# One add moved to VectorE, and GpSimd's work put in another order, in a hash-masked attention followed by a PReLU layer

## The chip, the cores and the metric

The kernel runs on one core of a Trainium2 chip. The metric is the device time of one launch in microseconds (us). A profile is one execution recorded by the hardware; its span runs from the first to the last instruction, and the launch's time is a little longer. The engines are named as in the profile: PE (TensorE, matrix products), DVE (VectorE), ACT (ScalarE), POOL (GpSimd), SP (SyncE, which here only starts transfers).

## What is computed

Attention with a hash mask, then a two-layer network with a PReLU between its products. Everything is float32.

```python
# q, k, v: (4, 8, 768, 64), proj: (64, 6)
q_bits = (einsum('bhsd,dk->bhsk', q, proj) > 0)
k_bits = (einsum('bhsd,dk->bhsk', k, proj) > 0)
mask   = bucket(q_bits)[:, :, :, None] == bucket(k_bits)[:, :, None, :]
scores = where(mask, q @ k.T / sqrt(64), -1e9)
attn   = softmax(scores)                # rows sum to 1
x      = (attn @ v) as (3072, 512)      # heads side by side
# w_in: (512, 2048), w_out: (2048, 512), alpha: (2048,)
h = x @ w_in
g = maximum(h, 0) + alpha * minimum(h, 0)
out = g @ w_out
```

## The kernel before

**The two parts.** `fast_path` has an attention part, up to about 336 us of the profile, and a dense part after it, where the two products are done with seven instead of eight block products each. The change is in the attention part alone.

**Attention by pairs.** The 32 heads of the batch are taken as 16 pairs (`NPAIR`), and the loop `for pi in range(NPAIR)` does one pair in each turn. The 768 keys are six tiles of 128 (`kc` from 0 to 5), the queries two groups of 384 columns (`g`), so that a pair has twelve cells. For a cell TensorE adds a product of the bits (bf16) and one of k and q (float32) into PSUM (L763), and ScalarE writes its exponential into the key tile `pts[kc]` (L766). There are only six such tiles, used anew by each pair. After the twelve cells TensorE multiplies them by v (`attend`, L796).

**The sums of the softmax.** The denominators are sums over all keys. The six key tiles, 1536 columns each, are first added together elementwise: `add_first` puts tiles 0 and 1 into `accp` (DVE, L774), `add_third` adds tile 2 to it (POOL, L782), `add_last` puts tiles 3, 4 and 5 into `accd` (DVE, L778 and L779), and `add_total` adds `accp` to `accd` (DVE, L785). Then `totals` multiplies `accd` by ones on TensorE (the tile `sm`, L810), which sums over the partitions. `divide` is called in the next pair's turn: DVE transposes the totals (L826), takes reciprocals into `rr` (L829), copies four blocks of 32 partitions by 12 columns between the quarters of the partitions (L832, L833), and, after a break in which `weight_begin` runs (clamp and shift of a piece of weights, L606 and L612, and `add_first`, L774), spreads the reciprocals by a transpose (`dn`, L837), multiplies (L843), and sends the result `x` to DRAM (`x_s`).

**The bits.** `hash_bits(pi + 1)` is called in pair `pi`'s turn: TensorE multiplies q and k by `proj` (L725), ScalarE takes the sign (L731), and six transfers issued from POOL's queue (L736, L738) bring the signs to the partitions where the next pair's scores want them.

**The weights.** Between these steps the weights are rounded, piece by piece, two pieces to a pair: ACT takes absolute values (L596, L600), DVE clamps (L606), shifts (L612), joins the sign (L637) and adds (L640). Four pieces of `w_in` make a group in a tile `wsi` with two buffers, and each group needs four sums of blocks (`weight_group`, POOL, L658), and then four transfers to DRAM (`w_in_s`, SP, L663). The sums and the store are put into the list `sums_due`, from which `weight_sums(count)` takes as many sums as its argument says, and a store where one comes first. It is called once in a pair, after `add_total`, with 2. There are four groups, so 16 sums; by the trace they run in pairs 3, 4, 6, 7, 9, 10, 12 and 13.

**Order.** Every engine works through its own queue in order. `do(...)` keeps an instruction in program order on its engine. Transfers aren't kept so: in pairs 9 and 12 the two sums stand between the bits' transfers in POOL's queue, in the other pairs ahead of all six.

Of the kernel before, what the change touches and what calls it, by code (L numbers as in the profile page):

```python
# [8 lines left out]
F32 = mybir.dt.float32  # L9
# [4 lines left out]
ALU = mybir.AluOpType  # L14
# [393 lines left out]
def fast_path(  # L408
# [13 lines left out]
    P = 128  # L422
# [20 lines left out]
    do = tc.keep_in_program_order  # L443
    PE, DVE, ACT, POOL = nc.tensor, nc.vector, nc.scalar, nc.gpsimd

    const = ctx.enter_context(tc.tile_pool(name="const", bufs=1))
# [8 lines left out]
    NPAIR = len(pairs)  # L455
# [25 lines left out]
    accp, accd, av, vsum, sums = {}, {}, {}, {}, {}  # L481
# [120 lines left out]
    def weight_clamp(i):  # L602
        if i < NW:
            i = order[i]
            x = wx[i]
            do(DVE.tensor_scalar(x, x, HI_MIN, None, op0=ALU.max, op1=ALU.max, accum_out=wmax[:, i : i + 1]))  # L606

    def weight_parts(i):
        i = order[i]
        x = wx[i].bitcast(U32)  # L610
        turned = i < HW and i % 4 == 3
        do(DVE.tensor_scalar(  # L612
            x, x, 3, 0x40000000 if turned else 0xC0000000, op0=ALU.logical_shift_left, op1=ALU.bitwise_xor,
        ))
# [27 lines left out]
    sums_due = []  # L642
# [24 lines left out]
            sums_due.append((one, (x[0], x[1], ALU.subtract, x[2])))  # L667
        sums_due.append((store, ()))

    def weight_sums(count):  # L670

        while sums_due and count:
            fn, x = sums_due.pop(0)
            count -= fn.__name__ == "one"
            fn(*x)


    def two_banks(name):
        return psum.tile([P, 2, 512], F32, name=name, tag="sc", bufs=3)
# [28 lines left out]
    def hash_bits(pi, halves=BOTH, engine=None):  # L708

        if halves.start == 0:
            bits["q", pi] = qbs[pi % 2]
            kb = pool.tile([P, 3 * CW], BF16, name=f"kb{pi}", tag="kb", bufs=1)
            bits["k", pi] = kb[:, :S]
            bits["raw", pi] = kb.rearrange("p (a w) -> p a w", w=CW)
        ps = {"k": two_banks(f"hs{pi}")}
        ps["q"] = psum_av.tile([P, 2, 512], F32, name=f"hsq{pi}", tag="av") if engine is DVE else ps["k"]
        for half in range(halves.start, halves.stop):
            for name in "qk" if engine is DVE else "kq":  # L720
                for s in range(2):
                    r, c = D * s, D * (s ^ half) + 32 * "kq".index(name)

                    for t, c in [("k", c)] + ([("q", c ^ D)] if engine is DVE and name == "q" else []):
                        do(PE.matmul(  # L725
                            ps[t][c : c + 32, half if t == "k" or engine is not DVE else 0, :CW], wh[r : r + D],
                            tr[name, pi][r : r + D, half * CW : (half + 1) * CW], start=True, stop=True,
                        ))
        if engine is None:
            raw = bits["raw", pi]  # L730
            do(ACT.activation(raw[:, 0:3:2], ps["k"][:, :, :CW], AF.Sign, bias=hb))  # L731
            for half in range(2):
                for s in range(2):
                    c = D * (s ^ half)
                    cols = slice(half * CW, (half + 1) * CW)
                    nc.gpsimd.dma_start(bits["q", pi][D * s : D * s + 32, cols], raw[c + 32 : c + 64, 2 * half])  # L736
                    if half:
                        nc.gpsimd.dma_start(bits["k", pi][D * s : D * s + D, cols], raw[c : c + D, 2])  # L738
            return
        for half in range(halves.start, halves.stop):  # L740
            cols = slice(half * CW, (half + 1) * CW)
            for s in range(2):
                c = D * (s ^ half ^ (engine is DVE)) + 32
                do(ACT.activation(
                    bits["q", pi][D * s : D * s + 32, cols], ps["q"][c : c + 32, 0 if engine is DVE else half, :CW], AF.Sign, bias=hb[c : c + 32],
                ))

            for to, c, n in [(0, 0, P)] if half == 0 else [(0, D, D), (D, 0, D)]:
                dst, src = bits["k", pi][to : to + n, cols], ps["k"][c : c + n, half, :CW]
                do(DVE.tensor_scalar(  # L750
                    dst, src, hb_k[c : c + n, 0:1], hb_k[c : c + n, 1:2], op0=ALU.is_gt, op1=ALU.subtract,
                ))
# [16 lines left out]
    def p(kc):  # L769
        return pts[kc].rearrange("p g s w -> p (g s) w")[:, :, :CW]  # L770

    def add_first(pi):
        accp[pi] = pool.tile([P, 2 * NCH, CW], F32, name=f"accp{pi}", tag="accp", bufs=1)
        do(DVE.tensor_tensor(accp[pi], p(0), p(1), op=ALU.add))  # L774
# [4 lines left out]
        do(DVE.tensor_tensor(accd[pi], accd[pi], p(5), op=ALU.add))  # L779

    def add_third(pi):
        do(POOL.tensor_tensor(accp[pi], accp[pi], p(2), op=ALU.add))  # L782

    def add_total(pi):
        do(DVE.tensor_tensor(accd[pi], accd[pi], accp[pi], op=ALU.add))  # L785
# [29 lines left out]
    def divide(pi, between=lambda: None):  # L815

        b, hp = pairs[pi]
        n = HW2 // 32  # L820
        a = pool.tile([P, NCH, HW2], F32, name=f"st{pi}", tag="st", bufs=1)
        r = pool.tile([P, NCH, n], F32, name=f"rc{pi}", tag="rc")
        rr = pool.tile([P, NCH, 2, n], F32, name=f"rr{pi}", tag="rr")
        d = pool.tile([P, NCH, CW], F32, name=f"dn{pi}", tag="dn", bufs=1)
        for g in range(NCH):
            do(DVE.transpose(a[:, g], sums[pi][:, g, :HW2]))  # L826
        do(DVE.tensor_scalar(r, a.rearrange("p g (n w) -> p g n w", w=32)[:, :, :, 0], S * EPS, None, op0=ALU.add))
        for h in range(2):
            do(DVE.reciprocal(rr[:, :, h], r))  # L829
        for q0 in (0, D):  # L830
            q1 = q0 + 32
            do(DVE.tensor_copy(rr[q0 : q0 + 32, :, 1], rr[q1 : q1 + 32, :, 1]))  # L832
            do(DVE.tensor_copy(rr[q1 : q1 + 32, :, 0], rr[q0 : q0 + 32, :, 0]))  # L833
        vsum[pi] = pool.tile([P, 1], F32, name=f"vs{pi}", tag="vs")
        do(DVE.tensor_scalar(vsum[pi], av[pi][:, 0, CW : CW + 1], EPS, None, op0=ALU.mult))
        between()
        do(DVE.transpose(  # L837
            d.rearrange("p g w -> p (g w)"),
            rr.rearrange("p g h n -> p (g h n)").unsqueeze(2).to_broadcast([P, 2 * NCH * n, 32]),
        ))  # L840

        x = mid.tile([P, NCH, CW], F32, name=f"x{pi}", tag="x", bufs=1)
        do(DVE.scalar_tensor_tensor(x, av[pi][:, :, :CW], vsum[pi], d, op0=ALU.add, op1=ALU.mult))  # L843
        nc.sync.dma_start(x_s[b, hp], x.rearrange("p g w -> p (g w)"))
# [316 lines left out]
    for pi in range(NPAIR):  # L1161
        i = 2 * pi

        def weight_begin():
            weight_clamp(i)
            weight_parts(i)
            add_first(pi)

        scores(pi, [c for c in CELLS if pi or c not in ahead])
        if pi:  # L1170
            divide(pi - 1, weight_begin)
        else:
            add_first(pi)
        weight_sum(i)
        weight_group(i)
        load_weight(i + 3)
        if pi == 0:
            weight_abs(1, DVE)
        weight_clamp(i + 1)
        add_third(pi)  # L1180
        add_last(pi)
        weight_parts(i + 1)
        weight_sum(i + 1)
        weight_group(i + 1)
        load_weight(i + 4)
        add_total(pi)
        weight_sums(2)
        if pi + 1 < NPAIR:
            hash_bits(pi + 1)
            if pi:  # L1190
                do(ACT.activation(tr["q", pi + 1], tr["q", pi + 1], AF.Copy, scale=DOWN))
        if pi + 2 < NPAIR:
            for name in "qk":
                (turn_blocks if name in BY_BLOCKS else turn)(pi + 2, name)
        attend(pi)
        if pi + 1 == NPAIR:
            now = ff1(0, 0)
            now.step(1)
        totals(pi)
        if pi + 1 == NPAIR:  # L1200
            now.step(5)
            divide(pi)
        else:
            weight_abs(i + 2)
        if pi + 2 < NPAIR:
            load(pi + 2, "v")
        if pi in (9, 11, 15):
            load_w((9, 11, 15).index(pi))
        if pi in (9, 10, 12):
            load_x(0, *{9: (0,), 10: (2, 3), 12: (1,)}[pi])  # L1210
        if 11 <= pi < 14 or pi == 15:
            sum_x(0, min(pi - 11, 3), DVE)
        if pi == 1:
            setup_alpha()
        for name in "qk":
            magnitude(pi, name)
            if pi + 3 < NPAIR:
                load(pi + 3, name)
        if pi + 1 < NPAIR:
            weight_abs(i + 3)  # L1220
# [97 lines left out]
```

## Time and profile before

| | us |
|---|---|
| median of 3 runs (891.02 to 896.54) | 891.14 |
| the profiled execution | 891.28 |
| its span | 889.4 |
| attention part, about | 336 |

| group (line, engine, what) | count | busy us | mean ns |
|---|---|---|---|
| L774 DVE, tiles 0 and 1 | 16 | 28.1 | 1758 |
| L782 POOL, tile 2 | 16 | 51.1 | 3194 |
| L778, L779 DVE, tiles 3 to 5 | 32 | 61.3 | 1963 and 1870 |
| L785 DVE, the total | 16 | 28.0 | 1751 |
| L658 POOL, sums of w_in | 16 | 29.3 | 1834 |
| L637 DVE, sign of the weights | 32 | 42.3 | 1322 |
| L736, L738 POOL, transfers of the bits | 90 | | about 500 each to issue |

The table's groups are sums over the whole span. [...] A row of the timeline gives start, duration, engine, line, operation, output and inputs with their shapes, the count, and in brackets the idle time before it with what ended it.

### The profile page before, as it was taken

The numbers are of one execution on the slowest core, as the hardware profiler recorded it, in microseconds if no ns is written. First come the engines' busy times: TensorE is split into PE (matmuls) and PEld (weight loads), VectorE is DVE, ScalarE is ACT, GpSimd is POOL, SyncE is SP. The second block draws the span as 40 slices with busy tenths as digits, with TensorE's granted clock in tenths as the row PEclk, the third lists the DMA queues.
The fourth block names the chain that finished last, engine by engine and source line by source line (L and its number), as shares of the span: only waits on it lengthen the run. The fifth ranks groups of instructions, "written<-read, shape, count | busy, mean of one in ns | idle before, by whom it ended". The sixth has DMA issues, their size and how long they took to land.

```text
span 889.4 us, 15185 instructions
## 1 busy us (share of the span) xinstructions
PE 864.7 (97%) x5718; PEld 577.0 (65%) x5718; DVE 766.4 (86%) x1262; ACT 370.1 (42%) x654; POOL 140.7 (16%) x152
## 2 busy tenths in 40 slices
PE   9999999998999999999999999999999999999996
PEld 4444444444444445558996558997557997557996
DVE  6999999998999987899898768898668988668986
ACT  7777677786787753221112222112222112222111
POOL 2334424434436311210000000000000000000000
PEclk9999999999999999999999999999999999999998
DMA  8665876867787616688334435434435343520242
GB/s 214 157 156 133 238 169 159 215 144 211 211 233 183 203 48 219 194 298 294 108 119 117 143 118 157 146 107 124 148 116 162 111 145 86 176 93 1 95 158 60
DMA packets 167683, 137.23 MB, mean 154 GB/s; under 512 B 122880, under 2 KB 151248, under 8 KB 164016
## 3 DMA queue, kind: packets, MB, share of 16 engines
q1 hardware_dynamic: 160000, 123.64, 47.6%
q0 software_dynamic: 5184, 11.34, 3.7%
q10 hardware_dynamic: 2416, 1.18, 0.5%
q8 instruction: 47, 0.77, 0.4%
q14 instruction: 36, 0.29, 0.1%
HBM read 104.87 MB, written 28.31 MB: 150 GB/s over the span
## 4 chain that ended last, share of the span: by engine, by line
PE 71%; DVE 12%; ACT 6%; issue 4%; DMA 3%; POOL 3%; SPq 0%; DVEq 0%; ACTq 0%; POOLq 0%
PE sc L763 7%; ACT pt L766 5%; PE av L796 4%; PE f_0a L896 2%; PE z_4a L896 2%; PE z_7a L896 2%; PE z_3a L896 2%; PE z_6a L896 2%; PE z_5a L896 2%; PE f_4a L896 2%; PE f_3a L896 2%; PE f_2a L896 2%; PE f_1a L896 2%; PE z_2a L896 2%; PE f_5a L896 2%
## 5 line engine op out<-in xcount | busy, mean ns | idle before, releaser
L766 ACT ACTIVATE pt<-sc 128x768 f32<-128x768 f32 x192 | 155.0, 812 | 42.0 <-PE sc L763 41.9
L763 PE MATMUL sc<-qT,kT 64*128 64x384 f32 x768 | 155.6, 483 | 0.0
L796 PE MATMUL av<-pt,vn 128*32 128x385 f32 (+1 forms) x1536 | 127.4, 486 | 0.0
L796 PEld LDWEIGHTS av<-pt,vn 128*32 128x32 f32 x1536 | 48.7, 109 | 77.4 <-issue 68.7
L763 PEld LDWEIGHTS sc<-qT,kT 64*128 64x128 f32 x768 | 69.1, 187 | 41.3 <-issue 39.9
L782 POOL TENSOR_TENSOR accp<-accp,pt 128x1536 f32<-128x1536 f32 x16 | 51.1, 3194 | 164.1 <-DVE accp L774 164.1
L763 PE MATMUL sc<-qb,kb 64*128 64x384 bf16 x384 | 64.9, 324 | 5.8 <-DMA qb<-kb 4.4
L949 DVE TENSOR_TENSOR g<-g,g 128x384 f32<-128x384 f32 x128 | 68.4, 555 | 2.2
L1013 DVE TENSOR_TENSOR gs<-g,gs 128x768 f32<-128x768 f32 x56 | 53.3, 952 | 1.0
L1005 DVE TENSOR_TENSOR ws<-wl 128x512 f32<-128x512 f32 x56 | 38.5, 687 | 18.1 <-DMA wl<-w_out_s 17.0
L1013 DVE TENSOR_TENSOR gs<-g 128x768 f32<-128x768 f32 x56 | 53.3, 951 | 0.0
L637 DVE SCALAR_TENSOR_TENSOR wx<-raw,wx 128x512 uint32<-128x512 uint32 x32 | 42.3, 1322 | 0.5
L945 DVE SCALAR_TENSOR_TENSOR g<-h,alpha 128x384 f32<-128x384 f32 x32 | 19.7, 616 | 25.2 <-ACT h L938 25.1
L763 PEld LDWEIGHTS <-kb 64*128 64x128 bf16 x384 | 20.0, 94 | 30.9 <-issue 4.6
L596 ACT ACTIVATE wr<-raw 128x512 int32<-128x512 uint32 x32 | 22.4, 701 | 32.4 <-issue 23.7
L774 DVE TENSOR_TENSOR accp<-pt,pt 128x1536 f32<-128x1536 f32 x16 | 28.1, 1758 | 8.5 <-ACT pt L766 8.2
L736 POOL DMA_DIRECT2D qb<-kb x60 | 30.2, 506 | 23.0 <-ACT kb L731 20.5
L779 DVE TENSOR_TENSOR accd<-accd,pt 128x1536 f32<-128x1536 f32 x16 | 29.9, 1870 | 2.0 <-ACT wr L596 0.5
L778 DVE TENSOR_TENSOR accd<-pt,pt 128x1536 f32<-128x1536 f32 x16 | 31.4, 1963 | 0.0
L658 POOL TENSOR_TENSOR wsi<-wsi 128x512 f32<-128x512 f32 x16 | 29.3, 1834 | 8.5 <-DVE wsi L640 8.0
L785 DVE TENSOR_TENSOR accd<-accd,accp 128x1536 f32<-128x1536 f32 x16 | 28.0, 1751 | 0.0
L896 PE MATMUL f_0a<-x,wi 128*128 128x384 f32 x64 | 23.5, 489 | 0.0
(352 smaller groups left out, 1749.8 us busy)
## 6 DMA issues: line engine op xcount, KB each, us to landing
wi<-w_in_s SPq DMA_DIRECT2D x32, 896.0 KB, 4.8
wl<-w_out_s SPq DMA_DIRECT2D x16, 1024.0 KB, 4.8
wl<-w_out_r SPq DMA_DIRECT2D x12, 1024.0 KB, 5.0
raw<-in_moe_w_out_dram SPq DMA_DIRECT2D x16, 512.0 KB, 4.6
raw<-in_moe_w_in_dram SPq DMA_DIRECT2D x16, 512.0 KB, 4.1
w_in_s<-wsi SPq DMA_DIRECT2D x16, 448.0 KB, 5.3
vn<-in_v_dram SPq DMA_DIRECT2D x16, 384.0 KB, 5.3
x_s<-x SPq DMA_DIRECT2D x16, 384.0 KB, 2.5
```

What stands on the lines that cost most here:

```text
L637: do(DVE.scalar_tensor_tensor(x.bitcast(U32), hi, 0x80000000, x.bitcast(U32), op0=ALU.bitwise_and, op1=ALU.bitwise_xor,))
L736: nc.gpsimd.dma_start(bits["q", pi][D * s : D * s + 32, cols], raw[c + 32 : c + 64, 2 * half])
L763: do(PE.matmul(sc[:, s, :CW], what["k", pi][r, ks], what["q", pi][r, qs], start=first, stop=not first,))
L766: do(ACT.activation(pts[kc][:, g, :, :CW], sc[:, :, :CW], AF.Exp, scale=SCALE / DOWN))
L778: do(DVE.tensor_tensor(accd[pi], p(3), p(4), op=ALU.add))
L779: do(DVE.tensor_tensor(accd[pi], accd[pi], p(5), op=ALU.add))
L782: do(POOL.tensor_tensor(accp[pi], accp[pi], p(2), op=ALU.add))
L796: do(PE.matmul(av[pi][D * s + t : D * s + t + 32, g, :w], nat["v", pi][:, s, kc * D + t : kc * D + t + 32], pts[kc][:, g, s, :w], start=(k ...
L896: do(PE.matmul(self.ps[bank], self.left(left, k), self.right(right, k), start=start and k == 0, stop=k == self.nk - 1, skip_group_check=no ...
L949: do(DVE.tensor_tensor(new_g(b, to)[:, i], g_m[b, x][:, i], g_m[b, y][:, i], op=ALU.subtract))
L1005: do(DVE.tensor_tensor(t, w2[b, n, x], w2[b, n, y], op=op))
L1013: do(DVE.tensor_tensor(t, g2[b, n, x], g2[b, n, y], op=ALU.subtract))
```

## The change

Three things are changed. Tile 2 of the keys is added to `accp` by VectorE instead of GpSimd. The four small copies of reciprocals go from VectorE to GpSimd. And the sums of `w_in` are taken one at a time, at two places: one after `hash_bits`, with a copy of one column of the pair's total (`late_sum`) put ahead of it, so that GpSimd doesn't begin before the total is there; the other in the next pair's `divide`, behind the copies of the reciprocals.

```diff
+    late_sum = const.tile([P, 1], F32, name="late_sum")
+
+    def weight_sums(count, after=None):
+
+        if sums_due and after is not None:
+            do(POOL.tensor_copy(late_sum, after[:, 0, :1]))
         while sums_due and count:
             fn, x = sums_due.pop(0)
             count -= fn.__name__ == "one"
             fn(*x)
...
     def add_third(pi):
-        do(POOL.tensor_tensor(accp[pi], accp[pi], p(2), op=ALU.add))
+        do(DVE.tensor_tensor(accp[pi], accp[pi], p(2), op=ALU.add))
...
         for q0 in (0, D):
             q1 = q0 + 32
-            do(DVE.tensor_copy(rr[q0 : q0 + 32, :, 1], rr[q1 : q1 + 32, :, 1]))
-            do(DVE.tensor_copy(rr[q1 : q1 + 32, :, 0], rr[q0 : q0 + 32, :, 0]))
+            do(POOL.tensor_copy(rr[q0 : q0 + 32, :, 1], rr[q1 : q1 + 32, :, 1]))
+            do(POOL.tensor_copy(rr[q1 : q1 + 32, :, 0], rr[q0 : q0 + 32, :, 0]))
+        weight_sums(1)
         vsum[pi] = pool.tile([P, 1], F32, name=f"vs{pi}", tag="vs")
...
         add_total(pi)
-        weight_sums(2)
         if pi + 1 < NPAIR:
             hash_bits(pi + 1)
+        weight_sums(1, accd[pi])
+        if pi + 1 < NPAIR:
             if pi:
                 do(ACT.activation(tr["q", pi + 1], tr["q", pi + 1], AF.Copy, scale=DOWN))
```

In the queues this gives: VectorE has 16 more adds of 1536 columns and 64 fewer copies; `add_third` stands on it between the second clamp (L606) and L778. GpSimd's queue has, for each pair, the six transfers of the bits, then `late_sum` and a sum, the four copies, a sum. The transfers on SP's queue are the same, with those of `w_in_s` about one pair later, and TensorE's and ScalarE's queues are the same. The lines named in the prediction are those of the kernel before.

More of the change, by code (lines that the diff above doesn't have):

```diff
@@ L668, in weight_group @@
         sums_due.append((store, ()))
-    def weight_sums(count):
+    late_sum = const.tile([P, 1], F32, name="late_sum")
+    def weight_sums(count, after=None):
+        if sums_due and after is not None:
+            do(POOL.tensor_copy(late_sum, after[:, 0, :1]))
         while sums_due and count:
```

## The prediction

> **What bounds the kernel now.** I read the page first: which engine is full, and what the chain that ended last is made of.
>
> ```profile
> PE 864.7 (97%) x5718; PEld 577.0 (65%) x5718; DVE 766.4 (86%) x1262; ACT 370.1 (42%) x654; POOL 140.7 (16%) x152
> ...
> PE 71%; DVE 12%; ACT 6%; issue 4%; DMA 3%; POOL 3%; SPq 0%; DVEq 0%; ACTq 0%; POOLq 0%
> ```
>
> TensorE leads, but the share is an average. The busy times by stage put PE at 545 of 554 us after 336 us (the dense part, which the change doesn't touch) and at some 95% (292 of 306 us) of the attention part from 30 us to there. So only attention can give time back. Next I asked for PE's waits between 0 and 345 us (in total, times, longest):
>
> ```profile
> PE sm L810 <- DVE accd L785: 8.9, 8, 1.5
> PE sc L763 <- DMA qb<-kb: 4.4, 2, 2.7
> PE sc L763 <- DVE st L826: 1.0, 2, 0.5
> ```
>
> The totals matmul (sm) waits for VectorE's pair total, and twice the scores wait for the bits' transfers. The timeline of VectorE in pair 4 shows why it is late (start, duration):
>
> ```profile
> 94.57 1.76 DVE L774 TENSOR_TENSOR accp<-pt,pt 128x1536 f32<-128x1536 f32 x1 [0.37 <-ACT pt L766]
> ...
> 98.19 2.02 DVE L637 SCALAR_TENSOR_TENSOR wx<-raw,wx 128x512 uint32<-128x512 uint32 x1
> 100.25 1.65 DVE L640 CUSTOM_DVE_ANT_0 wsi<-wx,wr 128x1024 uint16<-128x1024 uint16 x1
> ...
> 102.43 2.25 DVE L778 TENSOR_TENSOR accd<-pt,pt 128x1536 f32<-128x1536 f32 x1
> ...
> 106.91 0.69 DVE L637 SCALAR_TENSOR_TENSOR wx<-raw,wx 128x512 uint32<-128x512 uint32 x1
> 107.64 0.69 DVE L640 CUSTOM_DVE_ANT_0 wsi<-wx,wr 128x1024 uint16<-128x1024 uint16 x1
> 108.25 1.75 DVE L785 TENSOR_TENSOR accd<-accd,accp 128x1536 f32<-128x1536 f32 x1
> ```
>
> L637 and L640 take 0.69 us at their second call, and 2.02 and 1.65 at their first. GpSimd at the same times:
>
> ```profile
> 96.49 3.17 POOL L782 TENSOR_TENSOR accp<-accp,pt 128x1536 f32<-128x1536 f32 x1 [9.22 <-DVE accp L774]
> 99.63 3.44 POOL L658 TENSOR_TENSOR wsi<-wsi 128x512 f32<-128x512 f32 x2
> ```
>
> It works from 96.49 to 103.07, and each stretched VectorE instruction ends about 0.5 us after a GpSimd one. In pair 9 the sums stand among the bits' DMAs, and TensorE pays:
>
> ```profile
> 208.17 2.72 POOL L658 TENSOR_TENSOR wsi<-wsi 128x512 f32<-128x512 f32 x1 [2.63 <-DVE wsi L640]
> 210.85 0.52 POOL L736 DMA_DIRECT2D qb<-kb  x1
> ...
> 214.50 0.32 PE L763 MATMUL sc<-qb,kb 64*128 64x384 bf16 x1 [2.67 <-DMA qb<-kb]
> ```
>
> **What the skill says.** The Trainium skill, "SBUF — State Buffer", section "SBUF: two separate sides": VectorE and GpSimd share a pair of ports under an exclusive lock; a VectorE instruction in a two-port mode or with two SBUF inputs is blocked for as long as a GpSimd one holds it, and the other way round. The trace agrees: the two-input L637, L640 and L778 are stretched, while L606 (0.67 us at 101.82, under the second sum), the transposes L699 and L837, and L843, which reads PSUM, keep their times. "GPSIMD Engine Reference", 3.1, has GpSimd about twice as slow on a two-input add; here the same 1536 columns take 3.17 against 1.76 us.
>
> **The present period.** Starts of sm for pairs 0 to 15: 29.87, 49.10, 68.55, 89.43, 110.14, 129.41, 150.29, 171.01, 190.62, 209.90, 233.59, 252.84, 272.77, 295.49, 315.40, 335.36; 305.49 us for 15 periods. Where TensorE never waits, a period is 19.25 to 19.28. With sums in it, it is 20.7 to 20.9, and 23.7 and 22.7 after the two late transfers.
> When VectorE is late there is a loop: sm waits for L785; then come sm, four score cells and four exponentials (3.24) until L774 may start; then VectorE's chain to the next L785. From the trace: sm to L774 5.15 us (110.14 to 115.29), L774 to L785 12.23 in pairs without sums (195.77 to 208.00), L785 to sm 1.90. That is 19.28: **the loop is already as long as TensorE's own period**, so what VectorE gains or loses counts as soon as the loop is the longer.
>
> **The change part by part.**
> 1. The third add leaves GpSimd (16 x 3.18 us). L637 no longer waits for it: 2.05 to 0.69, a gain of 1.36 in each pair. In pair 0 it is L640 that waits (3.56 against 0.69, so 2.87).
> 2. The add comes to VectorE, ahead of L778. Independent adds follow each other at 1.67 to 1.68 (L774 to L837): +1.68. Net of 1: L774 to L785 becomes 12.23 - 1.36 + 1.68 = **12.55**, in sum pairs too, since no sum lies there any more (13.68 in pair 4).
> 3. Four copies of 32x12 leave VectorE (0.16 to 0.17 us each, 0.72 with gaps). They lie between sm and L774. VectorE's work from L785 to L774 is 6.69 us of 7.05 (pair 9: 0.36 idle), so without them it idles 1.08: I count **nothing**, as the exponentials end last. In pairs 12 to 14, L868 fills that slack (7.70 from L785 to L774), but there TensorE has itself been held by L826, which the copies follow; nothing again.
> 4. On GpSimd the trace has no such copy. From below: six memsets of 128x4 took 0.27, 0.05 each. From above: 1536 columns take 3.17 and 512 take 1.28, a line with 0.33 fixed; so 0.05 to 0.33 each, 1.3 for four. They start at 4.6 us after L785's start plus a hand-over of 0.16 (L774's end to L782), and L837, which now waits for them, comes at 8.7: hidden, 2.5 us to spare at the worst. In the last pair nothing stands between; up to 0.8 us, but PE runs the first dense products then.
> 5. The sums. The bits' six DMAs keep their order and now have no sum ahead of them, so the two transfers are not late: 4.4 us off PE. The wait (late_sum, a 128x1 copy) is queued behind those DMAs; behind it stand one sum, the four copies, the second sum, and then the next pair's DMAs, which wait for ScalarE's Sign ten us later anyway. (In pairs 5, 8, 11 and 14 only a store is left in the list, and the wait costs GpSimd nothing that anyone needs.) The first sum runs 0.3 to 1.6 us after L785's end, under the transposes L699, which don't need the lock. The second follows the copies, from about 5.2 to 6.1 us after L785's start, for 1.28. It meets L612 (due at 5.5, stretched like L827 under a sum at 212.06: 0.64 for 0.17) and perhaps the head of L774 (due at 7.05). Cost 0 to 0.4 us in each of the eight periods that hold sums (4, 5, 7, 8, 10, 11, 13, 14); below nothing there is no way. I take **0.2**.
> 6. The stores of w_in_s: the same 16 DMAs on SP, about one pair later, since the store stays in the list until the next call of weight_sums. SP waited 9.7 us for GpSimd at L663; now the sum is long done when the store comes up, so the loads queued behind aren't held. The staging tile has two buffers and each lasts some three pairs; the first reader of w_in_s (254.67) comes some 50 us after the second group's store. Nothing.
>
> **The sum.** Pair 0: L785 at 27.97 - 2.94 + 1.68 = 26.7, so sm follows the attention matmuls at 29.08 instead of 29.87 (-0.79). Periods after: 1: 19.58; 2: 19.74 (it holds the transpose of alpha, 5.31 instead of 5.15 from sm to L774); 3 to 11: 5.15 + 12.53 + 1.90 = 19.58 each (12.55 less rounding), 176.2; 12 to 14: 20.23 each (5.80 from sm to L774), 60.7; 15: 19.96, TensorE's own. Together 296.2, with 8 x 0.2 297.8; before 305.5. Gain 7.7 + 0.8 = **8.5 us**. It passes on in full, as the dense part is TensorE's. The profiled execution was 891.28 us (span 889.4 and 1.88 around it), 0.14 above the median of 891.14, so I take the gain off the median: **882.6 us**, span about 880.9. In the likeliest case 880.5 to 886.
>
> **Rivals.**
> *TensorE becomes the bound again.* If VectorE's chain comes out 0.3 us shorter, all periods fall to TensorE's 19.27 (19.9 in 12 to 15): gain 14, time 877. For it: the loop misses that by only 0.3. Against: every duration in the loop is steady to 0.02 us.
> *VectorE gives it back.* If the third add costs 1.85, as the dependent L778 to L779 does, and the second sum blocks L774 by 0.4, periods are 19.8 and 20.2: gain about 4, time 887; with a further 0.3 on each period, nothing. For it: VectorE is full in nearly all pairs. Against: the add's operands are old.
> *GpSimd's copies hold VectorE (slower).* If one copy between quarters of the partitions takes over 0.95 us, the four end after L837's due time, and every pair pays; at 1.5 us each 2.2 x 15 = 33 us on top of 882.6, 915; it is slower than before from 1.1 us each. For it: nothing like it is in the trace. Against: GpSimd's fixed 0.33.
> *The change doesn't part sums from transfers.* The wait could be satisfied early or the scheduler could move it; but late_sum reads the total, which VectorE writes only 2 us or more after the DMAs were issued (203.4 to 205.5, L785 until 209.8). Hardly.
>
> **How the numbers follow.** Chances: my forecast 0.60, TensorE's bound 0.12, given back 0.20, copies 0.08. The 1% bound, about what a measurement of this kernel can tell from no change, is 8.9 us, at 882.2: inside my likeliest case. So faster by over 1% is 0.42 (half the forecast and the first rival), within 1% is 0.49 (the other half and nearly all of what is given back), slower 0.09. The range, 878.5 to 889, leaves out most of the first rival and the worst of the others.
>
> **What would show it.** L637 at 0.69 on both calls and L640 never stretched; 32 adds with accp on VectorE at 1.76; sm waiting for L785 in nearly every pair but by 0.3 us, not 1.4; no PE wait on qb; idle before L774 grown to about 1 us; L658 at 1.3. It is wrong if the periods are below 19.4 or above 20 without L868, or if VectorE waits for a GpSimd copy at L837's place.

## The result, and the profile after

The changed kernel takes 881.32 us (median of 4 runs, 881.06 to 883.88). The kernel before had a median of 892.28 us in the same comparison (4 runs, 891.02 to 896.54). The ratio is 0.9875, with a 95% interval of 0.9836 to 0.9915: 0.85 to 1.64% faster. The profiled execution's span is 879.7 us, 9.7 less than before.

The changed kernel's lines are a little further down: the first add L774 is now L778, the third L782 is L786, L778 and L779 are L782 and L783, the total L785 is L789, sm L810 is L814, L826, L827 and L837 are L830, L831 and L842, L843 is L848. L606, L612, L637, L640 and L658 keep their numbers. The first group of the page:

```profile
PE 865.7 (98%) x5718; PEld 576.0 (65%) x5718; DVE 745.3 (85%) x1214; ACT 370.0 (42%) x654; POOL 96.2 (11%) x212
```

VectorE has taken over 28 us of adds and is busy for 21 us less than before. PE's waits in the first 345 us of the changed kernel (in total, times, longest):

```profile
PE sm L814 <- DVE accd L789: 3.4, 14, 0.3
PE sc L767 <- DVE st L830: 1.4, 3, 0.5
```

The wait on the bits' transfers is gone, and that of sm for the total has changed its form: 14 times 0.18 to 0.33 us in place of 8 times up to 1.5. VectorE's timeline in pair 4, the pair of the prediction, now reads so (start, duration; the last line is from pair 5's turn):

```profile
93.74 1.76 DVE L778 TENSOR_TENSOR accp<-pt,pt 128x1536 f32<-128x1536 f32 x1 [1.38 <-ACT pt L770]
...
97.36 0.68 DVE L637 SCALAR_TENSOR_TENSOR wx<-raw,wx 128x512 uint32<-128x512 uint32 x1
98.08 0.69 DVE L640 CUSTOM_DVE_ANT_0 wsi<-wx,wr 128x1024 uint16<-128x1024 uint16 x1
...
99.29 1.75 DVE L786 TENSOR_TENSOR accp<-accp,pt 128x1536 f32<-128x1536 f32 x1
100.96 1.75 DVE L782 TENSOR_TENSOR accd<-pt,pt 128x1536 f32<-128x1536 f32 x1
...
106.28 1.75 DVE L789 TENSOR_TENSOR accd<-accd,accp 128x1536 f32<-128x1536 f32 x1
...
111.52 0.43 DVE L612 TENSOR_SCALAR wx<-wx 128x512 uint32<-128x512 uint32 x1
```

Nothing is stretched, and from the first add to the total it is 12.54 us instead of 13.68. GpSimd's sums now lie beyond that stretch:

```profile
108.10 0.18 POOL L675 COPY late_sum<-accd 128x1 f32<-128x1 f32 x1 [3.58 <-DVE accd L789]
108.25 1.27 POOL L658 TENSOR_TENSOR wsi<-wsi 128x512 f32<-128x512 f32 x1
111.00 0.19 POOL L836 COPY rr<-rr 32x12 f32<-32x12 f32 x1 [1.49 <-DVE vs L840]
...
112.07 1.27 POOL L658 TENSOR_TENSOR wsi<-wsi 128x512 f32<-128x512 f32 x1
```

Periods, from the start of one sm to the next, in the traces (us):

| pair | before | after |
|---|---|---|
| 1, 2 | 19.23, 19.45 | 19.51, 19.75 |
| 3, 4, 6, 7 | 20.88, 20.71, 20.88, 20.72 | 19.58, 19.58, 19.59, 19.58 |
| 5, 8, 9, 11 | 19.27, 19.61, 19.28, 19.25 | 19.59, 19.59, 19.59, 19.58 |
| 10, 13 | 23.69, 22.72 | 19.58, 20.34 |
| 12, 14, 15 | 19.93, 19.91, 19.96 | 20.23, 20.32, 19.97 |
| sum | 305.49 | 296.38 |

So 9.1 of the 9.7 us come from the periods (0.1 from pair 0 and 0.5 from the dense part are the rest): 1.1 to 1.3 in each of pairs 3, 4, 6 and 7, which had sums in the chain, 4.1 and 2.4 in pairs 10 and 13, which had those and a late transfer, and **0.3 lost** in each of nearly all the others.

### The profile page after: what moved, and what is told of

Read it like the earlier page. It is cut to its first block, busy times and chain, and to the rows that moved or that the text cites. A ratio compares the mean times of both kernels' runs of the same rounds, so it can differ in the third digit from the quotient of the medians.

```text
span 879.7 us, 15201 instructions
## 1 busy us (share of the span) xinstructions
PE 865.7 (98%) x5718; PEld 576.0 (65%) x5718; DVE 745.3 (85%) x1214; ACT 370.0 (42%) x654; POOL 96.2 (11%) x212
## 4 chain that ended last, share of the span: by engine, by line
PE 66%; DVE 19%; issue 5%; DMA 4%; ACT 3%; SPq 1%; DVEq 0%; ACTq 0%
PE sc L767 3%; ACT pt L770 3%; DVE accd L789 3%; PE f_0a L901 2%; PE z_4a L901 2%; PE z_7a L901 2%; PE z_3a L901 2%; PE z_6a L901 2%; PE z_5a L901 2%; PE f_4a L901 2%; PE f_3a L901 2%; PE f_2a L901 2%; PE f_1a L901 2%; DVE accd L782 2%; DVE accp L786 2%
## 5 line engine op out<-in xcount | busy, mean ns | idle before, releaser
L778 DVE TENSOR_TENSOR accp<-pt,pt 128x1536 f32<-128x1536 f32 x16 | 28.3, 1770 | 21.2 <-ACT pt L770 21.2
L783 DVE TENSOR_TENSOR accd<-accd,pt 128x1536 f32<-128x1536 f32 x16 | 28.1, 1759 | 1.7
L786 DVE TENSOR_TENSOR accp<-accp,pt 128x1536 f32<-128x1536 f32 x16 | 28.0, 1753 | 0.0
L782 DVE TENSOR_TENSOR accd<-pt,pt 128x1536 f32<-128x1536 f32 x16 | 28.0, 1752 | 0.0
L789 DVE TENSOR_TENSOR accd<-accd,accp 128x1536 f32<-128x1536 f32 x16 | 28.0, 1751 | 0.0
L901 PE MATMUL f_4a<-x,wi 128*128 128x384 f32 x64 | 23.3, 486 | 0.0
L901 PE MATMUL f_1a<-x,wi 128*128 128x384 f32 x64 | 23.3, 486 | 0.0
```

Source lines behind the costliest of these rows:

```text
L782: do(DVE.tensor_tensor(accd[pi], p(3), p(4), op=ALU.add))
L786: do(DVE.tensor_tensor(accp[pi], accp[pi], p(2), op=ALU.add))
L901: do(PE.matmul(self.ps[bank], self.left(left, k), self.right(right, k), start=start and k == 0, stop=k == self.nk - 1, skip_group_check=no ...
```

## The experiments

The loop theory of the prediction says three things that can be tried apart: only what lies between the first add and the total counts on VectorE; the sums' new place is the gain; the add's move is a small loss. The experiments set other readings against it: one takes GpSimd's long add for the trouble, and another counts VectorE's load wherever it lies. In the comparisons of this section the kernel before, run on the same chip, had medians of 891.0 to 891.6 us.

**The add alone.** The kernel before, with only this edit:

```diff
     def add_third(pi):
-        do(POOL.tensor_tensor(accp[pi], accp[pi], p(2), op=ALU.add))
+        do(DVE.tensor_tensor(accp[pi], accp[pi], p(2), op=ALU.add))
```

> The kernel before with the third add alone moved to VectorE. Loop theory: where no sums run, the period (start of sm to start of sm) is 19.58 us (L774 to L785 12.55 instead of 12.23), 0.3 longer than before; where sums run they still stretch VectorE's adds by about 1.4 us in all, and in pairs 9 and 12 they still stand among the bits' transfers (PE waits 4 us in all). Time 890 to 895 us, no faster than before. Rival 'the long add was the trouble' (GpSimd's 3.2 us add blocked VectorE, taking it off is the gain): periods of at most 19.6 nearly everywhere, 881 to 884 us.

901.72 us, ratio 1.0111 (1.0083 to 1.0139): **slower** than before, and by more than the theory had reckoned. Most periods without sums are 19.51 to 19.58, as expected, but those of pairs 3 and 6 are 24.3. VectorE's timeline in pair 3 (lines of the kernel before; L782 is the third add):

```profile
79.45 2.46 DVE L782 TENSOR_TENSOR accp<-accp,pt 128x1536 f32<-128x1536 f32 x1
81.84 2.84 DVE L778 TENSOR_TENSOR accd<-pt,pt 128x1536 f32<-128x1536 f32 x1
84.78 2.66 DVE L779 TENSOR_TENSOR accd<-accd,pt 128x1536 f32<-128x1536 f32 x1
87.36 1.49 DVE L612 TENSOR_SCALAR wx<-wx 128x512 uint32<-128x512 uint32 x1
88.89 1.63 DVE L637 SCALAR_TENSOR_TENSOR wx<-raw,wx 128x512 uint32<-128x512 uint32 x1
```

And GpSimd's at the same time, where x2 merges two sums in a row:

```profile
79.02 4.05 POOL L658 TENSOR_TENSOR wsi<-wsi 128x512 f32<-128x512 f32 x2 [13.91 <-DVE wsi L640]
...
86.05 3.92 POOL L658 TENSOR_TENSOR wsi<-wsi 128x512 f32<-128x512 f32 x2
```

Five instructions in a row are stretched, 4.7 us over their usual times, and sm waits 4.94 us. The reader should see why there are four sums here and not two: in the kernel before, the next pair's sums were held back by the next pair's third add, which stood ahead of them in GpSimd's queue. With the add gone from that queue, they start as soon as the bits' transfers are issued, in the same chain. I had mentioned no such role of the add: it was a spacer.

The stretched instructions are not the whole loss. The period after, pair 4's, is 22.35 us, though no sum lies in it: from sm to the first add it takes 7.92 us instead of 5.15. TensorE's granted clock was 0.51 in the 6 us that begin with this late sm, and 1.00 in the 6 us after them. After pair 6, where sm waits 4.95 us, the clock was 0.50 again and these 5.15 us became 7.24. In the kernel before, the clock stayed at 1.00 after a wait of 2.67 us (pair 10). So a long wait of TensorE cost more than its own length here.

**All but the add.** The changed kernel with the third add back on GpSimd (the same edit the other way round).

> The changed kernel with the third add back on GpSimd. Loop theory: L637 is stretched again to 2.05 us, but 1.68 us of add leave the chain: L774 to L789 is 12.23, the loop 19.28, level with TensorE's own period; no stretched adds, no PE wait on the bits; pairs 12 to 14 19.9. So 15 periods of about 292 us instead of 296.4, less up to 0.8 in pair 0: 877.5 us, faster than the changed kernel by 3 to 4.5 us. Rival 'the long add was the trouble': back to 889 to 892 us.

878.67 us, ratio 0.9854 (0.9828 to 0.9881), as expected, and 2.65 below the changed kernel. Periods are 19.25 (19.63 in two), 19.92 to 19.98 in pairs 12 to 14, 292.5 together. L637 is stretched again, from 0.69 to 2.04, and these 1.35 us are cheaper than the add's 1.67. That GpSimd's long add was the trouble is refuted by these two runs.

**All but the copies.** The changed kernel with the four copies on VectorE:

```diff
-            do(POOL.tensor_copy(rr[q0 : q0 + 32, :, 1], rr[q1 : q1 + 32, :, 1]))
-            do(POOL.tensor_copy(rr[q1 : q1 + 32, :, 0], rr[q0 : q0 + 32, :, 0]))
+            do(DVE.tensor_copy(rr[q0 : q0 + 32, :, 1], rr[q1 : q1 + 32, :, 1]))
+            do(DVE.tensor_copy(rr[q1 : q1 + 32, :, 0], rr[q0 : q0 + 32, :, 0]))
```

> The changed kernel with the four copies back on VectorE. Loop theory: they lie in the 1.38 us of idle ahead of the first add, so periods stay at 19.58 to 19.6. But the second sum now follows the first at once and meets L868 in pairs 13 and 14: up to 1.2 us in each of those. Time 881.3 to 884 us. Rival 'VectorE's load': 0.72 us in each of 15 periods, 892 us.

882.37 us, ratio 0.9894 (0.9869 to 0.9919). Periods stay at 19.58 to 19.63, and only that of pair 14 grows by more than 0.1, from 20.32 to 21.30. So 0.72 us of work on VectorE in each pair cost nothing, as it lies in idle time.

**All but the wait.** `weight_sums(1, accd[pi])` becomes `weight_sums(1)`: the first sum stays behind the bits' transfers, but no longer waits for the total.

> The changed kernel without the copy that makes the first sum wait for the pair's total; the sum stays behind the bits' transfers in the queue. Loop theory: the sum starts as soon as the last transfer is issued, under L637 and L640 of the chain, and stretches one of them by about 1 us in pairs 3, 4, 6, 7, 10 and 13 (in 9 and 12 its group is complete only with the second L640, so that L789 keeps it off): 6 us, 887 us (885 to 889). Rival 'the place behind the transfers is enough': 881.3 us, periods of 19.58.

888.39 us, ratio 0.9962 (0.9949 to 0.9974). Six periods, those of pairs 3, 4, 6, 7, 10 and 13, are longer by 1.0 to 1.2 us, the others not. In pairs 3 and 6 it is L640 and L637 that are stretched, to 1.66 us each, as I had named them; in the other four it is the one ahead of them, L612. VectorE's timeline of this kernel in pair 4:

```profile
104.97 1.64 DVE L612 TENSOR_SCALAR wx<-wx 128x512 uint32<-128x512 uint32 x1
```

GpSimd's:

```profile
105.02 1.30 POOL L658 TENSOR_TENSOR wsi<-wsi 128x512 f32<-128x512 f32 x1
```

0.43 has become 1.64. TensorE waited for no transfer of the bits here. So with the other two parts of the change in place, the new places in the queue bring 3 us of the change's 10, and the wait for the total the other 7.

**A filler in the idle time, and in the chain.** An extra VectorE copy from PSUM, whose output is overwritten afterwards, was put into the changed kernel's `divide` at one of two places, in one kernel at the first added line, in the other at the second:

```diff
+        do(DVE.tensor_copy(d[:, 0], av[pi][:, 0, :CW]))
         between()
+        do(DVE.tensor_copy(d[:, 0], av[pi][:, 0, :CW]))
```

> The changed kernel with one more VectorE copy of 384 columns from PSUM into the tile dn (overwritten later), about 0.5 us (L848 has 768 columns from PSUM in 1.02, L830 192 in 0.34), put ahead of the weights' clamp, before the first add. PSUM input, so no lock. Loop theory: the 1.38 us idle ahead of the first add shrinks by 0.5, periods stay at 19.58 to 19.6, 881.3 us. Rival 'VectorE's load': 0.5 x 15, 888.5 us.

> The same copy put behind the first add, in the chain from L778 to L789. Loop theory: every period of 1 to 14 grows by the copy's 0.5 us to about 20.1, 888 us. Rival 'TensorE sets the period': 881.3 us.

One run each. Ahead of the first add: 881.61 us, periods of pairs 3 to 11 19.58 to 19.69. Behind it: 890.45 us, and the periods of pairs 1 to 14 grow by 0.64 to 0.67, most of them to 20.24 or 20.25 (the copy takes 0.55, and the transpose behind it, which writes the same tile, starts 0.66 after it). The same instruction costs 0.06 us a period at one place and 0.66 at the other. The first kernel also shows the edge of the idle time (VectorE, then GpSimd, in pair 5's turn):

```profile
111.42 1.53 DVE L612 TENSOR_SCALAR wx<-wx 128x512 uint32<-128x512 uint32 x1
112.87 1.75 DVE L778 TENSOR_TENSOR accp<-pt,pt 128x1536 f32<-128x1536 f32 x1
```

```profile
111.40 1.27 POOL L658 TENSOR_TENSOR wsi<-wsi 128x512 f32<-128x512 f32 x1
```

The filler pushes L612 under the second sum, which stretches it by 1.1; with the 0.46 from the filler's start to the next instruction's that is 0.2 more than the 1.39 us of idle, and the period is 0.08 longer.

**The sums alone.** The add and the copies as before, only the sums' new places and the wait.

> The sums' new places and the wait alone: the third add on GpSimd and the copies on VectorE, as in the kernel before. Loop theory: periods without sums 19.25 to 19.28; the second sum follows the first at once and stretches L831 by 0.5 us, of which about 0.36 is idle anyway: 19.3 to 19.5 in periods 4, 5, 7, 8, 10, 11, about 1 us more in one or both of 13 and 14, where L868 is met. 15 periods of about 294.5 us, 880.5 us: the sums' move alone gives more than the whole change. Rival 'the parts need one another' (without the add or the copies moved, the sums' new places bring little): above 886 us.

880.39 us, ratio 0.9874 (0.9845 to 0.9903). Periods 19.23 to 19.29 but for 2 (19.45, the transpose of alpha), 12 to 15 (19.92, 21.01, 20.97, 19.96). This one part brings as much as the whole change. The second sum, which follows the first at once here, stretches L831 to 0.55 in idle time, and L873 to about 2 us in pairs 13 and 14.

**The add split in two.** GpSimd does the first 768 columns of the third add, VectorE the others:

```diff
-        do(DVE.tensor_tensor(accp[pi], accp[pi], p(2), op=ALU.add))
+        for engine, h in ((POOL, slice(0, NCH)), (DVE, slice(NCH, 2 * NCH))):
+            do(engine.tensor_tensor(accp[pi][:, h], accp[pi][:, h], p(2)[:, h], op=ALU.add))
```

> The changed kernel with the third add split by columns: 768 on GpSimd, 768 on VectorE. Loop theory: GpSimd's half takes about 1.75 us from 1.9 after the first add's start and ends as L637 begins, so that L637 stays at 0.7 to 0.8; VectorE's half costs 0.88. L774 to L785 becomes 11.75 to 11.9, the loop 18.9, shorter than TensorE's 19.27, which now sets the period: 15 periods of 291.5 us, sm no longer waits for the total; 876.5 us. If VectorE's loop were still the bound: 19.58, 881.3 us.

**874.24 us, ratio 0.9801 (0.9777 to 0.9825)**: better than both kernels, 7 us below the changed one. GpSimd's timeline of this kernel in pair 6:

```profile
132.69 1.68 POOL L787 TENSOR_TENSOR accp<-accp,pt 128x768 f32<-128x768 f32 x1 [3.62 <-DVE accp L778]
```

VectorE's:

```profile
132.43 0.97 DVE L843 STREAM_TRANSPOSE dn<-rr 128x768 f32<-128x768 f32 x1
133.44 1.02 DVE L849 SCALAR_TENSOR_TENSOR x<-av,vs,dn 128x768 f32<-128x768 f32 x1
134.37 0.68 DVE L637 SCALAR_TENSOR_TENSOR wx<-raw,wx 128x512 uint32<-128x512 uint32 x1
...
136.30 0.95 DVE L787 TENSOR_TENSOR accp<-accp,pt 128x768 f32<-128x768 f32 x1
```

GpSimd's half ends at 134.37, the very moment L637 begins. The two instructions beside it (L843 and L849 here) keep the 0.97 and 1.02 us that they take elsewhere, so the half is hidden. Periods are 19.14 to 19.17 (19.30 in pair 2), 19.4 to 19.6 in pairs 12 to 14, and PE no longer waits for the total (between 60 and 240 us its list of waits is empty).

**The split with the filler in the chain**, to see whether TensorE is really the bound there.

> The split add with the extra copy in VectorE's chain, which took 0.66 us of each period where it stood in the changed kernel. Loop theory: with the split the loop is 5.15 + 11.73 + 1.90 = 18.8 us, below TensorE's 19.15; with the copy 19.44: periods 3 to 11 grow by 0.3 only, 12 to 14 by 0.65. 15 periods of 294 us, 879 us. If VectorE were still the bound in the split kernel: 0.66 in each, 299 us, 884 us; if TensorE had more room to hide it: 874 us.

881.18 us (one run); the periods of pairs 3 to 11 are 19.44 to 19.47, 0.3 longer and not 0.66, and those of 12 to 14 are 20.10 to 20.19; 294.6 together. The sum 5.15 + 11.73 + 0.66 + 1.90 is 19.44. So the split kernel's period of 19.15 hid about the first 0.36 us: something other than VectorE's chain sets it. That it is TensorE's own work is argued from its having no wait left there, not tried. The time is 2 us above the expected one: against the split kernel's run, sm of pair 0 came 0.4 us later, the dense part took 0.9 more, and the periods together are 0.6 above what I had expected.

The parts, put together (us); the medians stand in the same order as the sums of the periods:

| third add | copies | sums | median | 15 periods |
|---|---|---|---|---|
| GpSimd | VectorE | as before | 891.2 | 305.5 |
| VectorE | VectorE | as before | 901.7 | 316.7 |
| GpSimd | VectorE | moved | 880.4 | 293.9 |
| GpSimd | GpSimd | moved | 878.7 | 292.5 |
| VectorE | VectorE | moved | 882.4 | 297.4 |
| VectorE | GpSimd | moved, without the wait | 888.4 | 303.2 |
| VectorE | GpSimd | moved (the change) | 881.3 | 296.4 |
| split | GpSimd | moved | 874.2 | 289.2 |

So moving the sums brings 10.8 us with the add on GpSimd and 19.3 with it on VectorE (copies on VectorE in both). Moving the add costs 10.5 us where the sums stay, and 2.0 to 2.7 where they are moved. The copies' move brings 1.1 and 1.7 us by these medians, which is not much above the 0.6 by which the kernel before differs between comparisons.

## Why the prediction was right, point by point

The prediction was 882.6 us, the measurement 881.3: a gain of 8.5 forecast, and of 9.7 in the spans. Which side of 1% it would fall on was left nearly even, with a little more for within 1%. It fell beyond 1%, at 1.25%, but the interval, 0.85 to 1.64%, takes in both sides. The gain of the spans is made up of 9.1 from the periods (7.7 forecast), 0.1 from pair 0 (0.8 forecast) and 0.5 from the dense part (nothing forecast), so the sum is nearer than some of its terms, and that is luck.

- *The loop* held. Predicted 19.58 us a period, measured 19.58 to 19.59 (with the 12.55 of step 2 the sum would have been 19.60; I put 12.53 into it); 20.23 with L868, measured 20.23. The fillers show that it is a loop with idle time at one place and none at another.
- *L637* (step 1) is at 0.69 in both calls (687 ns on the mean of 32), and *the add* (step 2) costs 1.67: 12.55 predicted, 12.54 measured.
- *The copies* (step 3) brought nothing by themselves on VectorE: the idle time ahead of the first add went from 0.37 to 1.38. On GpSimd (step 4) they took 0.18 to 0.31 us, and the last of four 0.38 in pairs 0 and 1, a little over the upper bound; together they stayed within 1.1 us, below the 1.3. VectorE waited for them only in the last pair, 1.0 us where I had put up to 0.8. Their use is another: they hold the second sum back. With them, L612 has passed when the sum starts (111.52 to 111.95, and 112.07), and the sum ends at 113.34, when the first add starts, 113.33. That fit, 0.12 us clear on one side and none on the other, was not planned: it is luck. Without the copies pair 14 lost 1 us (and with the add on GpSimd, 13 and 14, 1 us each).
- *The sums* (step 5) were mis-sized on the safe side: 0.2 us in eight periods, 1.6 together. Measured: nothing in six, 0.1 in pairs 13 and 14, where L778 takes 1.85. I had L612 due at 5.5 us after the total's start; it comes at 5.24, just ahead of the sum, since without the copies VectorE's small instructions follow each other more closely.
- *Pair 0*: forecast was sm 0.79 us earlier, measured 0.11. The chain there did become shorter, 11.16 instead of 12.36. The sum forecast 11.10, with 2.94 for what L640 gives back; with the 2.87 of step 1 it is 11.17. In all six kernels with the whole add on VectorE, sm comes 13.28 or 13.29 us after the first add; in the three with it on GpSimd, 14.26 or 14.27. So this part gives about 1 us, more than I forecast. What hid it is the start of the first add, which lies anywhere between 15.61 and 16.57 us in the eleven profiles: 15.61 in that of before, 16.48 in that of after.
- *The stores* (step 6) cost nothing that shows in PE's waits. The dense part took 0.5 us less than before, 553.6 instead of 554.0. In the other profiles it lies between 553.4 and 555.0 (553.6 in that with the add alone, 555.0 in that with the sums alone), so half a microsecond is within its scatter and can't be put down to the change; what moves it stays open.
- *A wrong reading that did no harm*: I took 19.25 to 19.28 for TensorE's own period. The split add shows 19.15, so TensorE's is no longer than that. The periods of before without sums were already VectorE's loop, by 0.1 us, which the list of waits doesn't show. So the first rival's gain, had it come, would have been larger than 14 us.
- *A reading of the lines that holds only in part*: I wrote that each stretched instruction of pair 4 ends about 0.5 us after one of GpSimd's. L637 and L640 do (0.55 and 0.54). L778 ends at 104.68, 1.6 us after the second sum; it began 0.6 us before that sum's end and took 0.5 longer than alone.

Of the rivals, "VectorE gives it back" did not come: the third add costs 1.67 us and not 1.85, the second sum delays the first add's chain by 0.1 at most, and the 0.3 us a period that the add does cost was in the forecast. Neither slow copies nor an early end of the wait appeared.

## What to carry to other kernels

When two engines are nearly level, find the loop between them and write down where it has idle time: an instruction in the idle time costs nothing, the same one elsewhere costs its full length, as long as that loop is the longest one (in the split kernel it cost 0.3 of 0.66). For work on GpSimd the question is less how long it takes than which VectorE instructions it lies beside: put it under those that kept their times under it, and use a dependency to hold it there, since a place in the queue is no time. And before taking work off a queue, look at what stands behind it; it may have been what kept that apart.

## What the runs showed of the hardware

- The Trainium skill, "SBUF — State Buffer", section "SBUF: two separate sides", has VectorE and GpSimd excluding each other on a shared pair of ports. The runs agree, for tensor_scalar too: L612, with one SBUF input, went from 0.43 to 1.49, 1.53 and 1.64 us under a sum (in the add alone, the filler in the idle time and the kernel without the wait), while L606, also tensor_scalar but with an accumulated maximum, stayed at 0.67 (kernel before, at 101.82 us) under one.
- When the two contend again and again, much is lost. In the add alone, four sums that take 1.27 us each by themselves cost VectorE 4.7 us in five instructions, nearly the whole of the four (5.1).
- GpSimd's copy of 32x12 between quarters of the partitions took 0.18 to 0.19 us where another followed and 0.30 to 0.38 as the last of four (0.19 in the last pair); late_sum, one column, 0.18 to 0.19.
- After waits of 4.94 and 4.95 us TensorE's granted clock was 0.51 and 0.50 (the add alone, 93 to 99 us and 159.2 to 162 us); it was 1.00 after the wait of 2.67 us in the kernel before.
